# Opening part of an attention and two-MoE kernel: the sigmoids of a batch side by side, and a weight piece's last step behind the next piece's first

## The chip, the cores and the metric

One core of a Trainium2 chip runs the whole program. The metric is the device time of one execution in microseconds (us), taken as the median of several runs. The engines are named as the profile names them: PE (matrix products and transposes), ACT (activations and copies), DVE (elementwise work and reductions), POOL (elementwise work) and SP (it issues most DMAs).

## The reference

```python
def _attn_ref(q, k, v, M_prev, z_prev, beta):
    B, H, S, D = q.shape                       # 4, 8, 576, 64
    scores = np.matmul(q, k.transpose(0, 1, 3, 2)) / np.sqrt(D)   # causal mask, softmax -> a
    local = np.matmul(a, v)
    q_p = phi(q)                               # elu(q) + 1
    mem_out = einsum(q_p, M_prev) / (einsum(q_p, z_prev) + 1e-06)
    g = sigmoid(beta)
    return g * mem_out + (1 - g) * local

def _moe_ref(x, w_gate, w_val, w_out):         # x: 2304 x 512, weights 512 x 1536 and 1536 x 512
    return (sigmoid(x @ w_gate) * (x @ w_val)) @ w_out

def _moe2_ref(x, w_a, w_b, w_out):
    return ((x @ w_a) * (x @ w_b)) @ w_out

# out = moe2(moe(attention))
```

## The kernel before, in words

**Two parts.** The opening part (about the first 315 us) computes the attention for 16 pairs of heads, one pair after the other, and between the attention's instructions does part of the first MoE for the batches whose attention is done (`moe_a`, 4 of the 12 chunks of the hidden width). The late part computes the rest of both MoEs, with PE's order written out by hand. Its program is the same before and after the change.

**A pair.** The loop over `p` goes through a list of steps (`FIRST` for the first four pairs, `FIFTH`, then `LATER`). The steps that the text names are: the scores on PE (`scX`, `scY`, line 233); their masked copy with the row minimum on DVE (line 262) and the exponential on ACT (line 267), together `exX` and `exY`; transposes of q and k (line 180) with the copies out of PSUM, `kt` on ACT (line 176) and the put of `qt` on DVE (line 173); transposes of the probabilities (lines 368 and 380) with copies out of PSUM into `aw` on ACT (line 152); the product with v (`pv`, lines 398 and 404); and `M`, three or more products of the first MoE (lines 484 to 486, 492 to 494 after the change). All transposes and `pv` share three PSUM buffers named `tp`, so a copy out of PSUM that comes late holds PE. "Pair 4" below means the stretch on PE from the first score product of `p` = 4 to that of `p` = 5.

**The weights.** `w_stream` prepares 12 weight pieces of the first MoE, piece by piece. Each piece (`w_piece`) is a load of 512 KB into one of two buffers `st`, and then three steps: w1 (line 438 on DVE and 442 on ACT), w2 (lines 444 and 447 on DVE, then an integer add on POOL, line 450), and w3 (line 453 on ACT, which reads POOL's sum, then 454 on DVE, which reads ACT's result). Two buffers `wt` carry a piece from w1 to w3. A step `W` in the lists takes one step of the stream up to `p` = 3 and two from `p` = 4 on. The load of piece n+2 is issued in w3 of piece n.

**The sigmoids.** In `moe_a`, `gcopy` copies a chunk of the gate's product out of PSUM (line 527); after the fourth chunk two sigmoids of 128x1024 follow on ACT (line 530). The exponentials of the attention need another table of ACT, so a change of tables (`ACT_TABLE_LOAD`) stands before a sigmoid and again before the next exponential. `gat` (line 567) multiplies a chunk with its sigmoid.

**What sets the order.** In the opening part a scheduler orders each engine's instructions when the program is built, from the order of the code, its data dependencies and an estimate of when each instruction can run. Engines run their own list strictly in order.

Of the kernel before, what the change touches and what calls it, by code (L numbers as in the profile page):

```python
# [11 lines left out]
AF = mybir.ActivationFunctionType  # L12
# [7 lines left out]
def kernel(  # L20
# [31 lines left out]
    MA = 4  # L52
    PARTS = 9

    vec, act, pool, pe = nc.vector, nc.scalar, nc.gpsimd, nc.tensor
# [369 lines left out]
    def w_piece(wsrc, layer, c, kind, src):  # L425
        s = stp.tile([P, 512, 2], I32, tag="st", name="st")
        w32 = wsrc[kind].bitcast(I32)
        if kind == 2:
            nc.sync.dma_start(out=s.rearrange("p f t -> p (f t)"), in_=w32[c * P:(c + 1) * P, :])
        else:  # L430
            nc.sync.dma_start(
                out=s.rearrange("p (a f) t -> p a (f t)", a=KD),
                in_=w32[:, 2 * c * P:2 * (c + 1) * P].rearrange("(a p) f -> p a f", p=P),
            )
        yield
        hi, lo = s[:, :, 1], s[:, :, 0]
        c32 = work.tile([P, 512], I32, tag="wt", name="wt", bufs=NW)
        vec.tensor_scalar(
            out=c32.bitcast(F32), in0=hi.bitcast(F32), scalar1=2.0 ** -112, scalar2=None,
            op0=ALU.mult,  # L440
        )
        act.activation(out=lo, in_=lo.bitcast(U32), func=AF.Copy, scale=2.0 ** -29)
        yield
        vec.tensor_scalar(
            out=c32, in0=c32, scalar1=3, scalar2=None, op0=ALU.logical_shift_left
        )
        vec.scalar_tensor_tensor(
            out=c32, in0=hi, scalar=-(1 << 31), in1=c32, op0=ALU.bitwise_and, op1=ALU.bitwise_or
        )
        pool.tensor_tensor(out=c32, in0=c32, in1=lo, op=ALU.add)  # L450
        yield
        t = unit(src, f"w{kind}")
        act.activation(out=t[:, 0], in_=c32.bitcast(F32), func=AF.Copy)
        vec.tensor_tensor(
            out=t[:, 1], in0=c32.bitcast(F32), in1=t[:, 0].bitcast(F32), op=ALU.subtract
        )
        ws[layer, c, kind] = t
        yield

    def w_stream(pieces, ahead):  # L460

        gens = []
        pieces = iter(pieces)

        def more():
            a = next(pieces, None)
            if a is not None:
                g = w_piece(*a)
                next(g)
                gens.append(g)  # L470

        for _ in range(ahead):
            more()
        yield
        while gens:
            g = gens.pop(0)
            for i in range(3):
                next(g)
                if i == 2:
                    more()  # L480
                yield

    def mm3(o, w, ws_, xh, xl, first, last):
        pe.matmul(o, lhsT=w[:, 0, ws_], rhs=xh, start=first, stop=False, skip_group_check=True)  # L484
        pe.matmul(o, lhsT=w[:, 0, ws_], rhs=xl, start=False, stop=False, skip_group_check=True)  # L485
        return pe.matmul(  # L486
            o, lhsT=w[:, 1, ws_], rhs=xh, start=False, stop=last, skip_group_check=True
        )
# [16 lines left out]
    def moe_a(b):  # L505

        G, sg, gs, mo = {}, {}, {}, []  # L510

        def bank():
            return psm.tile([P, 512], F32, tag="m", name="m")

        def pairs():
            return work.tile([P, 2, 512], F32, tag="sg", name="sg", bufs=2)

        def half(c, kind, kk):
            if kk == 0:
                G[c] = bank()  # L520
            w, xs = ws[0, c, kind], xs_a[b, kk]
            mm3(G[c], w, slice(kk * P, kk * P + P), xs[:, 0], xs[:, 1], kk == 0, kk == KD - 1)

        def gcopy(c):
            if c % 2 == 0:
                sg[c // 2] = pairs()
            vec.tensor_copy(out=sg[c // 2][:, c % 2], in_=G[c])
            if c == MA - 1:
                for i in range(MA // 2):
                    act.activation(out=sg[i], in_=sg[i], func=AF.Sigmoid)  # L530

        def gat(c):
            gs[c] = gate(G[c], sg[c // 2][:, c % 2], 512)
            if c == MA - 1:
                finished.append(b)

        def outp(f, c):
            if c == 0:
                mo[:] = [bank()]
            mm3(mo[0], ws[0, c, 2], slice(f * P, f * P + P), *gs[c], c == 0, c == MA - 1)  # L540

        def fin(f):
            if f % 2 == 0:
                sg["io"] = pairs()
            io = sg["io"]
            if f % 2:
                act.activation(out=io[:, 1], in_=mo[0], func=AF.Copy)
                nc.sync.dma_start(out=x2d[b][:, f - 1:f + 1], in_=io)
            else:
                vec.tensor_copy(out=io[:, 0], in_=mo[0])  # L550

        for kind, then in ((0, gcopy), (1, gat)):
            for c in range(MA):
                for kk in range(KD):
                    yield (
                        b, (0, c, kind), partial(half, c, kind, kk),
                        partial(then, c) if kk == KD - 1 else None,
                    )
        for f in range(KD):
            for c in range(MA):  # L560
                yield (
                    b, (0, c, 2), partial(outp, f, c), partial(fin, f) if c == MA - 1 else None
                )

    def gate(vps, s, n, soon=False):

        st["gate"] = vec.tensor_tensor(
            out=s[:, 0:n], in0=vps[:, 0:n], in1=s[:, 0:n], op=ALU.mult
        )
        te = (dict(tag="gh", bufs=NG), dict(tag="gl", bufs=NG)) if NE is None else 2 * (dict(tag="e", bufs=NE),)  # L570
        gh = work.tile([P, 512], F32R, name="gh", **te[0])
        gl = work.tile([P, 512], F32R, name="gl", **te[1])
        rnd(gh[:, 0:n], s[:, 0:n], "g" in CD)
        (vec if soon else pool).tensor_tensor(
            out=gl[:, 0:n], in0=s[:, 0:n], in1=gh[:, 0:n].bitcast(F32), op=ALU.subtract
        )
        return gh, gl
# [43 lines left out]
    if True:  # L621
        start()
        wst = w_stream(
            [(w1, 0, c, kind, wp) for kind in range(3) for c in range(MA)],
            2,
# [1096 lines left out]
```

## Time and profile before

| what | value |
|---|---|
| median of 3 runs | 1053.35 us (1051.01 to 1054.12) |
| the profiled execution | 1052.07 us, of which its span is 1050.2 us |
| PE busy | 1025.6 us, 98% of the span |
| DVE, ACT, POOL busy | 736.7, 590.2, 188.8 us |
| granted clock of PE | 0.999 of full speed |

PE is the engine that the kernel's length hangs on. The 25 us by which it falls short of the span are the time that a faster order can win. Time on the other engines counts where PE waits for it.

### The profile page before, as it was taken

What the parts mean: (1) busy time and instruction counts of PE and PEld (TensorE: products, weight loads), DVE (VectorE), ACT (ScalarE), POOL (GpSimd) and SP (SyncE); (2) the same over time, 40 slices, a digit from 0 to 9 for tenths busy, and PEclk for the clock granted to TensorE, in tenths of its full rate; (3) what the DMA queues carried; (4) which work ended last, traced back from release to release, by engine and by line L of the source; (5) the groups of instructions that cost most, each with busy time, mean ns of one, the idle gap of its engine ahead of it and who ended that gap; (6) DMA issues with size and microseconds to landing.
All of it is one profiled execution on the core that took longest, in us unless ns stands there. A gap on an engine that the chain in (4) does not pass through costs nothing.

```text
span 1050.2 us, 17726 instructions
## 1 busy us (share of the span) xinstructions
PE 1025.6 (98%) x6158; PEld 859.0 (82%) x6158; DVE 736.7 (70%) x1589; ACT 590.2 (56%) x1276; POOL 188.8 (18%) x204
## 2 busy tenths in 40 slices
PE   7988999999999999999999999999999999999998
PEld 5656777777878988888888888888888888899998
DVE  6888755665627797765587558686586676898885
ACT  7888867867836556455654335454444545453432
POOL 2544521331211111110220000221121311000000
PEclk9999999999999999999999999999999999999999
DMA  7666434233215424332378754444352565644442
GB/s 174 155 180 161 135 89 125 81 87 85 60 54 172 161 82 149 102 130 79 118 267 285 237 169 161 130 136 136 95 190 91 189 231 182 216 141 143 144 125 72
DMA packets 154697, 150.14 MB, mean 143 GB/s; under 512 B 74608, under 2 KB 112624, under 8 KB 154608
## 3 DMA queue, kind: packets, MB, share of 16 engines
q1 hardware_dynamic: 152560, 148.16, 45.8%
q8 instruction: 48, 0.79, 0.3%
q10 hardware_dynamic: 2048, 0.86, 0.3%
q14 instruction: 41, 0.34, 0.1%
HBM read 103.29 MB, written 45.69 MB: 142 GB/s over the span
## 4 chain that ended last, share of the span: by engine, by line
PE 78%; DMA 6%; DVE 6%; ACT 5%; issue 2%; POOL 1%; SPq 1%; DVEq 0%; POOLq 0%; ACTq 0%
PE gv L485 16%; PE gv L486 16%; PE gv L484 16%; PE gv L1470 10%; PE m L484 3%; PE sc L233 3%; PE tp L404 3%; PE m L486 3%; PE m L485 3%; PE tp L368 2%; ACT s L267 1%; PE tp L398 1%; DMA xt<-xd 1%; PE tp L380 1%; DMA st<-in_moe_w_b_dram 1%
## 5 line engine op out<-in xcount | busy, mean ns | idle before, releaser
L484 PE MATMUL gv<-xm,w 128*128 128x512 f32 (+1 forms) x752 | 272.3, 362 | 0.5 <-ACT ev L1207 0.5
L486 PE MATMUL gv<-xm,w 128*128 128x512 f32 (+1 forms) x752 | 272.6, 363 | 0.0
L485 PE MATMUL gv<-xm,w 128*128 128x512 f32 (+1 forms) x752 | 272.6, 363 | 0.0
L925 POOL TENSOR_TENSOR wt<-wt,st 128x512 int32<-128x512 int32 x60 | 84.5, 1413 | 496.2 <-DVE wt L921 364.9
L484 PEld LDWEIGHTS gv<-xm,w 128*128 128x128 f32 x752 | 141.5, 188 | 23.4 <-ACT ev L1207 0.9
L485 PEld LDWEIGHTS gv<-xm,w 128*128 128x128 f32 x752 | 141.5, 188 | 22.6
L486 PEld LDWEIGHTS gv<-xm,w 128*128 128x128 f32 x752 | 141.6, 188 | 22.0
L1207 ACT ACTIVATE ev<-gv 128x512 f32<-128x512 f32 (+1 forms) x172 | 94.2, 562 | 79.4 <-PE gv L486 60.9
L1211 DVE TENSOR_TENSOR ev<-gv,ev 128x512 f32<-128x512 f32 x120 | 80.9, 684 | 64.4 <-PE gv L486 31.9
L1470 PE MATMUL gv<-wo,gs 128*128 128x256 f32 x1008 | 120.4, 282 | 0.5 <-DVE gs L1447 0.5
L1470 PEld LDWEIGHTS gv<-wo,gs 128*128 128x128 f32 x1008 | 120.2, 190 | 0.7 <-DVE gs L1447 0.7
L152 ACT ACTIVATE aw<-tp 128x512 f32<-128x512 f32 (+2 forms) x144 | 69.0, 507 | 46.3 <-PE tp L368 32.5
L262 DVE CUSTOM_DVE_ANT_0 s<-sc,mask 128x64 f32<-128x64 f32 (+4 forms) x160 | 69.0, 484 | 21.7 <-PE sc L233 21.6
L1446 ACT ACTIVATE gs<-ev 128x512 fp32r<-128x512 f32 (+1 forms) x96 | 50.9, 572 | 51.9 <-DMA ev<-gd 25.0
L915 ACT ACTIVATE wt<-st 128x512 f32<-128x512 f32 x60 | 39.7, 669 | 69.8 <-DMA st<-in_moe_w_out_dram 30.1
L267 ACT ACTIVATE s<-s,mx 128x320 f32<-128x320 f32 (+3 forms) x128 | 77.3, 607 | 2.7 <-DVE mx L262 2.7
L916 ACT ACTIVATE st<-st 128x512 int32<-128x512 uint32 x60 | 40.1, 669 | 37.8 <-DMA st<-in_moe_w_gate_dram 13.1
L486 PE MATMUL gv<-gs,w 128*128 128x512 f32 (+1 forms) x160 | 59.6, 373 | 0.0
L485 PE MATMUL gv<-gs,w 128*128 128x512 f32 (+1 forms) x160 | 59.4, 371 | 0.0
L484 PE MATMUL gv<-gs,w 128*128 128x512 f32 (+1 forms) x160 | 58.9, 368 | 0.0
L1447 DVE TENSOR_TENSOR gs<-ev,gs 128x512 fp32r<-128x512 f32 (+1 forms) x96 | 55.9, 615 | 3.1 <-ACT gs L1446 2.9
L233 PE MATMUL sc<-kt,qt 64*128 64x320 f32 (+4 forms) x468 | 54.2, 359 | 3.4 <-DVE mx L262 3.0
(158 smaller groups left out, 1828.5 us busy)
## 6 DMA issues: line engine op xcount, KB each, us to landing
gd<-ev SPq DMA_DIRECT2D x80, 256.0 KB
ev<-gd SPq DMA_DIRECT2D x80, 256.0 KB
st<-in_moe_w_out_dram SPq DMA_DIRECT2D x24, 512.0 KB
st<-in_moe_w_gate_dram SPq DMA_DIRECT2D x12, 512.0 KB
st<-in_moe_w_val_dram SPq DMA_DIRECT2D x12, 512.0 KB
st<-in_moe_w_a_dram SPq DMA_DIRECT2D x12, 512.0 KB
st<-in_moe_w_b_dram SPq DMA_DIRECT2D x12, 512.0 KB
x<-rd SPq DMA_DIRECT2D x32, 144.0 KB
```

Of the source, the lines that this page charges most:

```text
L152: act.activation(out=out, in_=src, func=AF.Copy)
L233: st["anchor"] = pe.matmul(scs[e][:, SC0[i] + a:SC0[i] + z], lhsT=x, rhs=y, start=n == 0, stop=n == len(terms) - 1, skip_group_check=True,)
L262: st["pace"] = vec.tensor_tensor_reduce(out=s, in0=scs[e][:, SC0[i]:SC0[i] + w], in1=mask[:, c:c + w], scale=1.0, scalar=BIG, op0=ALU.add, ...
L267: st["apace"] = act.activation(out=o, in_=s, func=AF.Exp, scale=-1.0, bias=mx[:, i:i + 1], accum_out=sms[p % 2][:, i:i + 1, e],)
L484: pe.matmul(o, lhsT=w[:, 0, ws_], rhs=xh, start=first, stop=False, skip_group_check=True)
L485: pe.matmul(o, lhsT=w[:, 0, ws_], rhs=xl, start=False, stop=False, skip_group_check=True)
L486: return pe.matmul(o, lhsT=w[:, 1, ws_], rhs=xh, start=False, stop=last, skip_group_check=True)
L925: pool.tensor_tensor(out=c32, in0=c32, in1=lo, op=ALU.add)
L1207: act.activation(out=t[:, 0:n], in_=src[:, 0:n], func=func)
L1211: st["gate"] = vec.tensor_tensor(out=t, in0=src, in1=t, op=ALU.add)
L1447: vec.tensor_tensor(out=t[:, 1, 0:n], in0=f[:, 0:n], in1=t[:, 0, 0:n].bitcast(F32), op=ALU.subtract,)
L1470: st["gate"] = pe.matmul(mo[i][:, 256 * r:256 * r + 256], lhsT=t[:, th, q_], rhs=w[:, wl_, wc:wc + 256], start=first and not r and not z, ...
```

## The change

Two edits. The first: after the fourth `gcopy` of a batch, the first of the two sigmoids now also waits for that `gcopy`, so that both stand next to each other. The second: `w_stream` yields its steps in another order. Before it was w1, w2, w3 of piece n, then of piece n+1. Now it is w1(0), w2(0), then w1(n+1), w3(n) with the load of n+2, w2(n+1) for each n. There are 37 steps in both.

```diff
         for _ in range(ahead):
             more()
         yield
+
+        for i in (0, 1):
+            next(gens[0])
+            yield
         while gens:
             g = gens.pop(0)
-            for i in range(3):
-                next(g)
-                if i == 2:
-                    more()
+            if gens:
+                next(gens[0])
+                yield
+            next(g)
+            more()
+            yield
+            if gens:
+                next(gens[0])
                 yield
...
-            vec.tensor_copy(out=sg[c // 2][:, c % 2], in_=G[c])
+            last = vec.tensor_copy(out=sg[c // 2][:, c % 2], in_=G[c])
             if c == MA - 1:
+
                 for i in range(MA // 2):
-                    act.activation(out=sg[i], in_=sg[i], func=AF.Sigmoid)
+                    a = act.activation(out=sg[i], in_=sg[i], func=AF.Sigmoid)
+                    if i < MA // 2 - 1:
+                        tc.add_manual_dep(
+                            a.ins, last.ins.name,
+                            mybir.DependencyInfo(
+                                mybir.DependencyClass.Sync, mybir.DependencyReason.DATA
+                            ),
+                            reason="one table",
+                        )
```

**What moves.** The built programs hold the same instructions on every engine, but for six `ACT_TABLE_LOAD` fewer on ACT (three before a sigmoid, three before an exponential). The order differs in the first 7 pairs, and for ACT also around the sigmoids of the two later batches; behind that all lists are the same. Lines above 480 have another number after the change (530 becomes 539, 527 becomes 535, 503 becomes 511).

ACT around the first sigmoid of the first batch, at the seam of pairs 5 and 6, before the change (`sg` is the gate, `mix` the first exponential of the next pair):

```order
L152 ACTIVATE aw<-tp 128x320 x2
L284 ACTIVATE e<-e 128x640
L152 ACTIVATE aw<-tp 128x512
L530 ACT_TABLE_LOAD
L530 ACTIVATE sg<-sg 128x1024
L267 ACT_TABLE_LOAD
L267 ACTIVATE mix,sm_93<-s_1355,mx 128x64
```

ACT after the change, in pair 6, where the second sigmoid of the batch stood before:

```order
L442 ACTIVATE st<-st 128x512
L176 ACTIVATE kt<-tp 128x448
L152 ACTIVATE aw<-tp 128x320
L539 ACT_TABLE_LOAD
L539 ACTIVATE sg<-sg 128x1024 x2
L152 ACTIVATE aw<-tp 128x320
L284 ACT_TABLE_LOAD
```

The first sigmoid and its two changes of tables have left the seam of the pairs; the two sigmoids stand between one pair of changes in pair 6, ahead of an `aw` copy.

DVE in pair 4 at `exY`, before the change (`w_977` is the weight piece whose w3 this is):

```order
L438 TENSOR_SCALAR wt<-st 128x512
L503 TENSOR_TENSOR xs<-x,xs 128x512
L454 TENSOR_TENSOR w_977<-wt,w_977 128x512
L262 ISA s,mx<-sc,mask 128x192
```

The same place after the change (the piece's number is now `w_980`), from the end of `exY` on:

```order
L262 ISA s,mx<-sc,mask 128x576
L262 ISA mx 128x1
L444 TENSOR_SCALAR wt<-wt 128x512
L300 TENSOR_REDUCE nr<-e 128x10
L454 TENSOR_TENSOR w_980<-wt,w_980 128x512
L173 TENSOR_SCALAR qt<-tp 128x448
L447 SCALAR_TENSOR_TENSOR wt<-st,wt 128x512
```

The w3 that stood in front of `exY` now stands behind it, between w2's first operation and the put of `qt`.

DVE in pair 5 behind `exY`, before the change:

```order
L262 ISA s,mx<-sc,mask 128x576
L262 ISA mx 128x1
L300 TENSOR_REDUCE nr<-e 128x10
L438 TENSOR_SCALAR wt<-st 128x512
L173 TENSOR_SCALAR qt<-tp 128x448
```

And after it:

```order
L300 TENSOR_REDUCE nr<-e 128x10
L535 COPY sg<-m 128x512
L438 TENSOR_SCALAR wt<-st 128x512
L173 TENSOR_SCALAR qt<-tp 128x448
```

A `gcopy` that stood ahead of `exY` now stands behind it, ahead of the put of `qt`.

## Rows read from the trace of the kernel before

**Rows 1.** The page's span, and its busy time of each engine.

```profile
span 1050.2 us, 17726 instructions
PE 1025.6 (98%) x6158; PEld 859.0 (82%) x6158; DVE 736.7 (70%) x1589; ACT 590.2 (56%) x1276; POOL 188.8 (18%) x204
```

**Rows 2.** Stretches of 25 us: length, then busy time of each engine.

```profile
core 0: us, PE busy (x) PEld busy (x) DVE busy (x) ACT busy (x) POOL busy (x), PEclk, DMA share, GB/s
50.00:75.00 25.00, 21.81 (x181) 14.68 (x177) 21.68 (x70) 21.83 (x62) 11.15 (x15) 1.00 0.67 178
75.00:100.00 25.00, 20.93 (x142) 14.89 (x139) 20.16 (x52) 20.57 (x53) 11.76 (x14) 1.00 0.64 170
100.00:125.00 25.00, 24.16 (x167) 18.33 (x167) 19.56 (x56) 22.51 (x54) 11.06 (x12) 1.00 0.51 142
125.00:150.00 25.00, 25.00 (x167) 19.52 (x166) 19.05 (x54) 18.84 (x53) 10.57 (x14) 1.00 0.35 98
```

**Rows 3.** The same view, cut at the pairs' first score products: pairs 2 to 7.

```profile
29.06:42.24 13.18, 11.06 (x87) 7.45 (x86) 10.87 (x36) 11.17 (x34) 6.30 (x8) 1.00 0.66 155
42.24:54.67 12.43, 11.75 (x101) 8.36 (x100) 10.95 (x36) 11.72 (x36) 5.71 (x8) 1.00 0.66 161
54.67:69.76 15.09, 12.58 (x102) 8.53 (x102) 12.38 (x42) 14.40 (x42) 5.72 (x10) 1.00 0.69 181
69.76:89.69 19.93, 17.32 (x119) 12.04 (x118) 18.44 (x50) 14.52 (x39) 10.78 (x11) 1.00 0.67 188
89.69:112.55 22.86, 20.88 (x147) 15.94 (x146) 18.69 (x53) 20.95 (x46) 10.31 (x12) 1.00 0.53 144
112.55:132.20 19.65, 19.34 (x134) 14.71 (x133) 14.47 (x39) 16.71 (x45) 10.27 (x12) 1.00 0.45 126
```

**Rows 4.** PE's timeline: start, length, what; in brackets idle time before it.

```profile
34.75 1.57 PE L233 MATMUL sc<-kt,qt 64*128 64x192 f32 x12 [0.84 <-DVE mx L262]
...
69.18 0.66 PE L368 MATMUL tp<-ident,s 128*128 128x128 f32 x4 [1.15 <-DVE qt L173]
...
80.20 0.49 PE L485 MATMUL m<-xs,w 128*128 128x512 f32 x1 [0.94 <-DVE xs L503]
...
89.10 0.66 PE L380 MATMUL tp<-ident,mix 128*128 128x128 f32 x4 [1.30 <-DVE qt L173]
...
96.25 0.76 PE L398 MATMUL tp<-aw,mv 128*64 128x320 f32 x4 [1.45 <-ACT aw L152]
...
114.65 0.33 PE L180 MATMUL tp<-ident,kn 128*128 128x128 f32 x1 [0.31 <-ACT aw L152]
```

**Rows 5.** ACT's timeline in pairs 5 and 6, and its group of loads before sigmoids.

```profile
74.45 0.63 ACT L453 ACTIVATE w<-wt 128x512 fp32r<-128x512 f32 x1 [2.43 <-POOL wt L450]
...
91.28 1.28 ACT L530 ACT_TABLE_LOAD   x1
92.58 1.06 ACT L530 ACTIVATE sg<-sg 128x1024 f32<-128x1024 f32 x1
93.65 1.28 ACT L267 ACT_TABLE_LOAD   x1
94.95 0.35 ACT L267 ACTIVATE mix<-s,mx 128x64 f32<-128x64 f32 x1
...
L530 ACT ACT_TABLE_LOAD x6 | 7.7, 1283 | 0.1
```

**Rows 6.** Weight steps on DVE and POOL, and a weight load on SP's queue.

```profile
64.57 0.69 DVE L454 TENSOR_TENSOR w<-wt,w 128x512 fp32r<-128x512 f32 x1 [1.78 <-ACT w L453]
83.23 1.46 DVE L447 SCALAR_TENSOR_TENSOR wt<-st,wt 128x512 int32<-128x512 int32 x1
109.74 0.74 DVE L438 TENSOR_SCALAR wt<-st 128x512 f32<-128x512 f32 x1 [0.26 <-DMA st<-in_moe_w_out_dram]
...
82.86 1.29 POOL L450 TENSOR_TENSOR wt<-wt,st 128x512 int32<-128x512 int32 x1
...
105.94 0.36 SPq L429 DMA_DIRECT2D st<-in_moe_w_out_dram x1
```

## The prediction

> **What bounds the kernel now.** I read the page first. PE is busy 1025.6 of 1050.2 us [rows 1], so over the whole program some 25 us are to be won at most, whatever the other engines save. Then the busy times by stretch, to see where those 25 us lie. From 125 us on PE is busy 25.00 of 25.00; in 50 to 125 us it is idle for 3.19, 4.07 and 0.84 us, together 8.1 [rows 2]. Cut at the pairs the same view gives PE's idle time as 2.12, 0.68, 2.51, 2.61, 1.98 and 0.31 us in pairs 2 to 7 [rows 3]. No engine is full there: in pair 4 ACT is busy 14.40 of 15.09 us, in pair 5 DVE 18.44 of 19.93, in pair 6 ACT 20.95 of 22.86 [rows 3]. So pairs 2 to 6 are bound by chains of waits that go from engine to engine, and from pair 7 on by PE alone.
>
> Then PE's own timeline, for what ended each idle time. Six of them carry the argument: 0.84 us at 34.75 for the score copies on DVE, 1.15 at 69.18 and 1.30 at 89.10 for the put of `qt` on DVE, 0.94 at 80.20 for a split on DVE, 1.45 at 96.25 and 0.31 at 114.65 for `aw` copies on ACT [rows 4]. Last the engines that were late. ACT idled 2.43 us at 74.45 in front of w3, until POOL's sum came; and at 91.28 to 94.95 it changed tables, did a sigmoid and changed back before the first exponential of pair 6 could start [rows 5]. DVE idled 1.78 us at 64.57 in front of its half of a w3, with `exY` of pair 4 queued behind [rows 6]. The change touches these three places.
>
> **The change part by part.** The sum is made against the profiled execution, 1052.07 us, which is 1.28 below the median of the runs shown, so I subtract it from the median at the end.
>
> The instructions are the same but for six changes of tables. At 1.283 us each [rows 5] ACT gets 7.7 us of free time. Four of the six belong to the second and third batch, which fall behind 125 us, where PE idles nowhere and ACT is busy 18.84 of 25 us [rows 2]. PE's own products hide those, and I count them as nothing; without that cover they would be worth 2.57 us for each batch. The first sigmoid of those batches now comes up to 1.06 us nearer to the product that needs it; the same cover holds, and I take nothing there too.
>
> *Pair 2.* The new order puts DVE's half of w3 behind `exX` and not in front. It takes 0.69 us, as the one at 64.57 [rows 6]. PE's idle 0.84 us at 34.75 ended on just these copies. I take 0.6 us; the bounds are 0 (another copy is late instead) and 0.84.
>
> *Pair 4.* The w3 that waited 1.78 us now stands behind `exY` on DVE, so `exY` and the put of `qt` behind it come earlier, and PE's 1.15 us at 69.18 should go. But ACT has only 15.09 - 14.40 = 0.69 us free in this pair, and what is late next is its `aw` copy. I take 0.5 us; the bounds are 0 and 1.15.
>
> *Pair 5.* With w2 and w3 of a piece no longer in one `W`, POOL has the time of another step for its sum, and ACT's 2.43 us go. The split behind it (0.94 us of PE at 80.20) comes in time. The 1.30 us at 89.10 stay, and grow: a `gcopy`, one DVE pass over 128x512 like w3 (0.69), now stands ahead of the put of `qt`, and PE's transposes of `mix` wait for that put with 12 products behind them. I take 0.94 - 0.69, some 0.3 us. The bounds are -0.7 (only the new wait) and 0.94 + 1.30 = 2.24.
>
> *Pair 6.* The seam loses two changes and a sigmoid, 1.28 + 1.06 + 1.28 = 3.62 us [rows 5], ahead of the first exponential. PE's wait of 1.45 us at 96.25 is for an `aw` copy behind them, and goes. The other end of the pair gets 1.06 us more in front of an `aw` copy, since two sigmoids stand between the changes there. ACT comes to that place with the 3.62 us in hand, but PE comes earlier as well, so I take the wait of 0.31 at 114.65 as little changed, some 0.05 more. That gives 1.4 us; the bounds are 1.45 - 1.06 = 0.4 and 1.45 + 0.31 = 1.8.
>
> The load of a weight piece is issued at the w3 of the piece two before it, as before, but w1 of its own piece now comes two steps later and not four, which from pair 4 on is one `W` and not two. The nearest row is the last load: issued at 105.94, and w1 at 109.74 still waited 0.26 us for it [rows 6], so a load takes 3.8 us. A pair has three or four `W` in 15 to 23 us [rows 3], some 5 us each. The load fits with about 1 us to spare, and I count it as nothing; what it costs if not is a rival below. SP no longer has to wait for POOL at that load, since the buffer is free a step earlier; no wait of SP shows on PE, so this too is nothing.
>
> Sum: 0.6 + 0.5 + 0.3 + 1.4 = 2.8 us, with -0.3 and 6.0 as the sums of the bounds. The late part has the same order on each engine and starts from the same tiles, so it only shifts. 1052.07 - 2.8 = 1049.3 for an execution like the profiled one, 1053.35 - 2.8 = 1050.55 for the median.
>
> The Trainium skill, ScalarE: Activation LUTs, section What ACT_TABLE_LOAD costs, counts about 2.66 us for a switch, 1.28 for the load and 1.38 for a drain. By that figure the seam would lose 6.4 and not 3.62 us, ACT would have 2.8 us more in hand, and the first rival below would be the likeliest, with its 1047.4. The trace disagrees: the load begins at 91.28 and the sigmoid at 92.58, and no second part lies between them or ahead of the load [rows 5].
>
> **The rivals.**
>
> *Most of PE's idle time goes.* ACT and DVE run ahead by their freed waits (2.43 and 1.78 us) and by the 3.62 us of the seam, and each next pair finds its copies done. For it: no engine is full in pairs 5 and 6. Against it: the put behind `gcopy`, and ACT in pair 4. At most 2.51 + 2.61 + 1.98 = 7.1 us [rows 3]; I take 6, which gives 1047.4.
>
> *The gain is given back by POOL.* An operation on DVE next to a POOL add takes longer: the w2 at 83.23 took 1.46 us with the add of 82.86 to 84.15 running [rows 6], against the 0.69 of a w3 alone. Before, w3(n) waited for the add of its own piece, so it never ran beside it. Now w3(n) stands right behind w2(n+1) on DVE, whose add starts on POOL just then: so in pairs 2, 4, 5 and 6, once each. That is up to 4 x 0.77 = 3.1 us on DVE, and it cancels the 2.8: 1053.6, no change. Against it: where DVE's next operation waits anyway, nothing is lost. The Trainium skill, SBUF — State Buffer, section Who interferes with whom, has the reason: a DVE operation with two inputs in SBUF and a POOL operation that reads SBUF keep each other out for a whole instruction. The trace agrees in that one row.
>
> *Slower: w1 waits for its load.* The lead is one `W`. Where the load is late, DVE stands still in w1, and behind it in order stand a w3 and `exX` of the next pair. DVE has 19.93 - 18.44 = 1.49 us free in pair 5 [rows 3]; beyond that PE waits. Three w1 stand in that stretch; at 1.5 us late each they hold DVE 4.5 us, which puts PE back by 3.0 and takes the gains of pairs 5 and 6 as well: 1053.35 - 1.1 + 3.0 = 1055.3. It decides from a load of some 5.5 us on, against the 3.8 seen. Against it: loads before had two `W`, and only one of them was waited for.
>
> **How the numbers follow.** The forecast, a gain of 1.5 to 4.2 us around 2.8 (1049.1 to 1051.9), gets 0.45. Most idle time gone: 0.20. Given back: 0.25. Slower: 0.10. About 0.3% (3.2 us) is what a measurement can tell from no change. The first rival lies beyond it, and so does somewhat under half of the forecast's range, 0.2, together 0.40 for faster. Slower by that much is the larger half of the last rival and the tail of the one before it, 0.09. The rest, 0.51, is within. The range for 8 in 10 reaches from most of the first rival, 1047.0, to beyond no change, 1054.6; it leaves out about 0.1 on either side.
>
> **What would show it.** In the profile after: three loads of tables in front of sigmoids and not six; no wait of ACT for POOL's sum near 2.4 us; pair 4's `exY` on DVE ending about 2 us earlier; the first exponential of pair 6 about 3 us or more earlier; PE's idle of 1.45 us before `pv` gone; a wait of about 2 us for the put of `qt` in pair 5; and the first score product of pair 8 some 2.8 us before 132.20. It is wrong if w1 on DVE shows waits for its DMA, if w3 on DVE takes 1.4 us in most places, or if behind 132 us the shift grows or is lost.

## The result and the profile after

The changed kernel took 1058.46 us (median of 6 runs, 1056.87 to 1059.42) against 1053.03 us (6 runs) of the kernel before on the same chip: a ratio of 1.0057, 95% interval 1.0046 to 1.0067, so 5.4 us slower. The prediction said 1050.55, in a range that ended at 1054.6, and gave "slower" 0.09.

The page after, the lines that answer to [rows 1]:

```profile
span 1057.2 us, 17716 instructions
PE 1030.4 (97%) x6158; PEld 862.8 (82%) x6158; DVE 736.7 (70%) x1589; ACT 582.5 (55%) x1270; POOL 188.7 (18%) x204
```

ACT lost the 7.7 us of six table loads, as costed. PE is busy 4.8 us longer with the same 6158 instructions, which points to time at a lower clock. The stretches after, cut as [rows 3] into pairs 2 to 7 (the third number from the end is the granted clock), then a part of pair 5, then pairs 8 to 14 together:

```profile
29.21:42.02 12.81, 11.01 (x87) 7.45 (x86) 10.40 (x35) 10.79 (x33) 5.71 (x8) 1.00 0.72 187
42.02:55.26 13.24, 12.09 (x103) 8.57 (x102) 12.62 (x41) 12.50 (x38) 6.01 (x9) 1.00 0.53 127
55.26:70.63 15.37, 12.56 (x100) 8.33 (x100) 13.52 (x42) 13.56 (x40) 7.34 (x10) 1.00 0.70 186
70.63:94.63 24.00, 19.77 (x122) 14.59 (x121) 20.49 (x52) 16.40 (x43) 10.07 (x12) 0.86 0.59 162
94.63:116.94 22.31, 20.83 (x138) 15.90 (x137) 16.58 (x45) 15.62 (x39) 8.67 (x11) 1.00 0.47 123
116.94:137.76 20.82, 20.82 (x139) 15.42 (x138) 14.70 (x41) 17.83 (x45) 11.12 (x13) 1.00 0.47 130
...
78.64:85.47 6.83, 5.79 (x18) 4.70 (x19) 6.64 (x17) 5.00 (x17) 2.17 (x3) 0.50 0.74 174
...
137.76:274.85 137.09, 136.67 (x1011) 106.16 (x1010) 81.22 (x258) 93.48 (x261) 34.90 (x52) 1.00 0.34 94
```

The same stretch in the kernel before:

```profile
132.22:269.31 137.09, 136.67 (x1009) 106.16 (x1009) 81.03 (x258) 99.61 (x266) 34.88 (x52) 1.00 0.34 94
```

Set against [rows 3], pairs 2 to 7 changed by -0.37, +0.81, +0.28, +4.07, -0.55 and +1.17 us, together +5.41. Pairs 8 to 14 are 137.09 us in both, so in the opening part everything happened before pair 8. Behind pair 14, where the order is the same, the two profiles differ by another 1.46 us (780.89 and 782.35); two profiles of one and the same program differ as much there (780.89 and, in e4 below, 779.54), so I read nothing from that part.

In this profile most of the loss is in pair 5; a second profile of the same program (e3 below) spreads it otherwise. In pair 5 PE is idle 24.00 - 19.77 = 4.23 us instead of 2.61, and busy 2.45 us longer. Pairs 6 and 7 do not hold the same work in both kernels: PE has 138 and 139 instructions there after the change and had 147 and 134 before, so these two are better taken together (+0.62).

What PE waited for in pair 5, from the timelines of PE, DVE, ACT and POOL after (start, length, what; idle time in brackets):

```profile
79.68 0.90 PE L368 MATMUL tp<-ident,s 128*128 128x128 f32 x3 [3.60 <-DVE qt L173]
80.80 0.63 PE L493 MATMUL m<-xs,w 128*128 128x512 f32 x1
81.23 0.63 PE L494 MATMUL m<-xs,w 128*128 128x512 f32 x1
...
73.97 1.90 DVE L287 SCALAR_TENSOR_TENSOR qp<-qn,e 128x640 f32<-128x640 f32 x1 [0.51 <-POOL mix L326]
...
77.01 1.17 DVE L454 TENSOR_TENSOR w<-wt,w 128x512 fp32r<-128x512 f32 x1 [0.78 <-ACT w L453]
78.10 0.21 DVE L262 CUSTOM_DVE_ANT_0 s<-sc,mask 128x64 f32<-128x64 f32 x1
...
79.34 0.28 DVE L173 TENSOR_SCALAR qt<-tp 128x128 f32<-128x128 f32 x1
...
75.79 0.67 ACT L442 ACTIVATE st<-st 128x512 int32<-128x512 uint32 x1 [3.08 <-DMA st<-in_moe_w_val_dram]
...
73.90 1.28 POOL L450 TENSOR_TENSOR wt<-wt,st 128x512 int32<-128x512 int32 x1
76.01 1.62 POOL L290 TENSOR_TENSOR e<-qp,zb 128x640 f32<-128x640 f32 x1 [0.82 <-issue]
```

The same place before, on DVE:

```profile
73.18 0.22 DVE L262 CUSTOM_DVE_ANT_0 s<-sc,mask 128x64 f32<-128x64 f32 x1
...
75.73 0.28 DVE L173 TENSOR_SCALAR qt<-tp 128x128 f32<-128x128 f32 x1
...
76.49 0.81 DVE L287 SCALAR_TENSOR_TENSOR qp<-qn,e 128x640 f32<-128x640 f32 x1
```

Before, DVE did `exX` and the put of `qt` (128 columns) first, and `qp` and w1 behind them. After, `qp`, w1 and a w3 stand ahead of `exX` in DVE's list. The put comes 79.34 - 70.63 = 8.71 us into the pair and not 75.73 - 69.76 = 5.97, and PE, whose MoE products now stand behind the transposes that need that buffer, idles 3.60 us. From 78.64, some 2.6 us into that wait, the granted clock is 0.50 (1.2 GHz) for 6.83 us: products follow each other in 0.43 us (80.80 to 81.23) and not in 0.23 as before.

The chain of waits in that place (start, length, what):

```profile
69.70 1.52 POOL wt L450
...
71.24 4.47 DMA st<-in_moe_w_val_dram
...
75.79 0.67 ACT st L442
...
77.01 1.17 DVE w L454
...
79.42 0.21 DVE qt L173
```

It reads like the third rival: a weight load that starts when POOL's sum frees its buffer, and w1 (here ACT's half) waiting 3.08 us for it. That was my first theory (A, in later runs L), and it fell. Its rival B, that the order of the steps itself costs, was made more precise on the way: P for PE's order, D for DVE's and ACT's.

### The profile page after: what moved, and what is told of

Read it like the earlier page. It is cut to its first block, busy times and chain, and to the rows that moved or that the text cites. A ratio compares the mean times of both kernels' runs of the same rounds, so it can differ in the third digit from the quotient of the medians.

```text
span 1057.2 us, 17716 instructions
## 1 busy us (share of the span) xinstructions
PE 1030.4 (97%) x6158; PEld 862.8 (82%) x6158; DVE 736.7 (70%) x1589; ACT 582.5 (55%) x1270; POOL 188.7 (18%) x204
## 4 chain that ended last, share of the span: by engine, by line
PE 79%; DVE 6%; DMA 5%; ACT 5%; issue 2%; SPq 2%; POOL 1%; ACTq 0%; DVEq 0%; POOLq 0%
PE gv L494 16%; PE gv L493 16%; PE gv L492 16%; PE gv L1487 8%; PE m L492 3%; PE m L494 3%; PE m L493 3%; PE sc L233 3%; PE tp L368 3%; PE tp L404 3%; ACT s L267 2%; PE tp L398 1%; DMA ev<-gd 1%; DMA xt<-xd 1%; PE tp L380 1%
```

## The experiments

"Before" is the median of the kernel before in the same set of runs; its level differs by up to 1 us from set to set, so the ratios are what to compare.

| run | median | before | ratio, 95% interval |
|---|---|---|---|
| e1 sigmoids only | 1052.11 | 1051.83 | 1.0003 (0.9995 to 1.0012) |
| e2 stream only | 1056.66 | 1051.83 | 1.0045 (1.0031 to 1.0059) |
| e3 load issued earlier | 1057.56 | 1051.83 | 1.0052 (1.0039 to 1.0066) |
| e4 before, load issued later | 1051.45 | 1051.83 | 0.9999 (0.9990 to 1.0007) |
| e5 third buffer | 1057.14 | 1052.42 | 1.0042 (1.0029 to 1.0055) |
| e6 after, PE's order of before | 1055.23 | 1052.42 | 1.0022 (1.0010 to 1.0033) |
| e7 before, PE's order of after | 1054.51 | 1052.42 | 1.0020 (1.0009 to 1.0031) |
| e8 gap filled | 1060.44 | 1052.42 | 1.0072 (1.0055 to 1.0088) |
| e9 after, scores' chain first | 1055.27 | 1051.34 | 1.0036 (1.0023 to 1.0049) |
| e10 as e9, and PE in pair 5 | 1055.50 | 1051.34 | 1.0041 (1.0028 to 1.0054) |
| e11 before, scores' chain late | 1054.09 | 1051.34 | 1.0025 (1.0017 to 1.0034) |
| e12 before, sigmoids held | 1052.12 | 1051.34 | 1.0001 (0.9992 to 1.0010) |
| e13 before, moves as costed | 1050.10 | 1052.54 | 0.9984 (0.9975 to 0.9992) |
| e14 as e13, copies ahead | 1051.60 | 1052.54 | 0.9992 (0.9983 to 1.0000) |
| e15 as e14, puts ahead | 1050.40 | 1052.54 | 0.9978 (0.9968 to 0.9987) |
| e16 as e9, scores together | 1055.52 | 1052.54 | 1.0029 (1.0019 to 1.0039) |
| e17 as e13, puts ahead | 1049.03 | 1052.03 | 0.9979 (0.9969 to 0.9989) |

**Which edit: e1 and e2.** Each is one hunk of the change's diff alone.

> Only the first edit: the two sigmoids of a batch side by side, the weight stream in the order of before. Theory A (in the new stream a weight piece's load has a lead of one W and not two, w1 waits for it on ACT and DVE, PE idles 3.6 us in pair 5 and then runs at a lower clock): the loss is not here, and the seam of pairs 5 and 6 gives what pair 6 gave after the change or my forecast of it, 0.5 to 1.4 us, so 1051.6 to 1052.5 against 1053.0. Rival C (two sigmoids in one place hold ACT 1.06 us longer in front of an aw copy, and PE's products slip behind transposes): the loss of 5.4 us shows here, 1056 to 1058.5.

> Only the second edit: the weight stream in the new order, the sigmoids as before. Theory A (lead of one W): the whole loss and none of the seam's gain, 1058.5 to 1060, with PE's idle time of about 3.6 us in pair 5 and a stretch at the lower clock behind it. Rival B (the order of the three steps itself costs, w3 next to POOL's add and ahead of the copies): the same 1058.5 to 1060, this run does not tell A from B. Rival C (the sigmoids): 1052 to 1054.

The loss is the stream's (e2 has 4.8 of 5.4 us, by medians), and C falls. e2 lies below the range that A and B shared, though its interval overlaps that of the change. The sigmoids alone gained nothing either. Pairs 6 and 7 of e1:

```profile
90.03:110.96 20.93, 20.41 (x143) 15.52 (x142) 17.52 (x52) 17.01 (x43) 10.15 (x12) 1.00 0.54 153
110.96:133.25 22.29, 20.95 (x138) 15.49 (x137) 15.24 (x40) 18.40 (x46) 10.82 (x12) 1.00 0.43 115
```

Pair 6 is 1.93 us shorter than in [rows 3], more than the 1.4 costed, and pair 7 is 2.64 longer. Part of both is that four of PE's transposes went from the end of pair 6 into pair 7 (143 and 138 instructions, not 147 and 134). In pair 7 PE waits for a put that waited for ACT's `kt` copy:

```profile
121.41 0.55 PE L368 MATMUL tp<-ident,s 128*128 128x128 f32 x3 [1.34 <-DVE qt L173]
```

**The load's lead: e3, e4 and e5.**

```diff
         for i in (0, 1):
             next(gens[0])
+            if i:
+                more()
             yield
...
             next(g)
-            more()
             yield
             if gens:
                 next(gens[0])
+                more()
                 yield
```

> Both edits, but the load of piece n+2 is issued right behind w2 of piece n, two steps earlier than after the change, so that the lead is again four steps (two W). Steps and their order are those after the change. Theory A (the lead): the wait of 3 us of ACT and DVE for the load in front of w1 goes, PE's 3.6 us in pair 5 and the slow stretch too, and the forecast of the prediction comes up: 1050.5 to 1052.5. Rival B (the order of the steps): the load changes nothing, 1057 to 1058.5. Between them a load that SP now issues while it waits for POOL's add, with other transfers queued behind it: 1053 to 1056.

> The kernel before with one thing changed: the load of piece n+2 is issued in w2 of piece n+1 and not in w3 of piece n, two steps later, so that w1 has a lead of one W as after the change. Order of the steps and sigmoids as before. Theory A (the lead): w1 waits for its load here too, PE idles in pairs 4 to 7, 1055.5 to 1059. Rival B (the order of the steps): within 1 us of before, 1052 to 1054.

Neither tells anything about the lead: the built programs are those of after (e3) and of before (e4), instruction for instruction on every engine. Here the scheduler issues a load when its buffer is free, wherever the code asks for it. They stand as second measurements of the two kernels, and as such they show something that one profile cannot. In e4 the kernel before repeats its pairs: none of pairs 2 to 7 differs from [rows 3] by more than 0.04 us. In e3 the changed kernel does not. Its pairs 2 to 5:

```profile
29.37:43.38 14.01, 12.15 (x86) 8.36 (x85) 11.33 (x39) 11.82 (x35) 6.31 (x9) 0.92 0.66 172
43.38:57.16 13.78, 12.62 (x103) 8.96 (x102) 11.75 (x36) 11.62 (x36) 5.33 (x8) 0.96 0.55 138
57.16:73.21 16.05, 13.22 (x100) 8.84 (x99) 14.19 (x42) 14.24 (x41) 7.93 (x10) 0.96 0.63 172
73.21:96.39 23.18, 19.83 (x122) 14.47 (x121) 20.86 (x52) 15.83 (x42) 9.55 (x11) 0.88 0.56 163
```

Against [rows 3] that is +0.83, +1.35, +0.96 and +3.25 us. Pair 5 is again the largest, but 3.1 us lie ahead of it, where the profile after had 0.7. The granted clock was 0.50 in three stretches of 3.41 us (from 41.08, 71.80 and 82.04), two of them at places where it stayed at 1.00 in the profile after. So a difference of a microsecond in one pair of the changed kernel, between two single profiles, says little.

What sets the lead is the buffer, so e5 gave every third piece a buffer of its own:

```diff
-        s = stp.tile([P, 512, 2], I32, tag="st", name="st")
+        nst[0] += 1
+        if nst[0] % 3:
+            s = stp.tile([P, 512, 2], I32, tag="st", name="st")
+        else:
+            s = work.tile([P, 512, 2], I32, tag="st3", name="st", bufs=1)
...
-            2,
+            3,
```

> Both edits, and every third weight piece of the opening is loaded into a third buffer st, with three loads ahead, so that a load no longer waits for POOL's sum of the piece before last. Theory L (w1 waits for its load, because in the new order the buffer comes free only three steps before the w1 that needs it): the waits of ACT and DVE for st in pair 5 go, the put of qt there comes 1.5 to 3 us earlier, pair 5 shrinks from 24.0 to 20.5 to 22 us, 1054 to 1056. Theory P (the order that the scheduler gives PE after the change is at fault: in pair 5 nine products of the MoE that stood ahead of or between the transposes stand behind the first three of them): the load wait goes, but PE still idles for the put, 1056 to 1058.5.

ACT and DVE in pair 5 of e5, which begins at 71.92:

```profile
76.05 0.64 ACT L458 ACTIVATE w<-wt 128x512 fp32r<-128x512 f32 x1 [1.92 <-POOL wt L455]
...
76.96 2.03 DVE L459 TENSOR_TENSOR w<-wt,w 128x512 fp32r<-128x512 f32 x1
...
80.15 0.28 DVE L173 TENSOR_SCALAR qt<-tp 128x128 f32<-128x128 f32 x1
```

No wait for `st` is left there. But the next instruction of the same list waits 1.92 us for POOL's sum, DVE's w3 runs 2.03 us beside a POOL operation, and the put still comes 8.23 us into the pair. The time is in the range of P, and A falls: the load was only the wait that ended last among several on instructions that now stand ahead of `exX`.

**PE's order: e6 and e7.** A chain of dependencies holds PE's 284 instructions between pairs 3 and 7 in a given order; in e6 the changed kernel gets the order of before, in e7 the kernel before gets that of after. Only PE is held: in answer the scheduler also moved some copies, puts and weight steps on ACT and DVE in that stretch, so neither run changes PE's order alone.

```diff
+        turn = [pes[a + k] for a, n in PE_ORDER for k in range(n)]
+        for a, b in zip(turn, turn[1:]):
+            tc.add_manual_dep(b, a.name, ...)
```

> Both edits, but PE's instructions in pairs 3 to 7 are held in exactly the order that they had before the change; the other engines keep the new streams, except where the scheduler now places an instruction a little otherwise. Theory P (PE's order): pair 5 comes back to 20 to 21.5 us, no slow clock, and the gains of the forecast show: 1050.5 to 1053.5. Theory L (the load): DVE's put of qt stays at its late place, nine products of 0.23 us fill 2.1 of PE's 3.6 us, the rest stays idle: 1055 to 1057.

> The kernel before, but PE's instructions in pairs 3 to 7 are held in exactly the order that they have after the change; weight stream and sigmoids are those of before. Theory P (PE's order): most of the loss without either edit, 1054.5 to 1058. Theory L (the load): the put of qt in pair 5 is as early as before, so PE loses at most 1 us there: 1051.5 to 1053.

Pair 5 of e6 and PE's wait in it, then pairs 3, 5 and 6 of e7 and PE's longest wait in its pair 5:

```profile
71.15:92.22 21.07, 18.19 (x118) 13.27 (x117) 19.26 (x49) 14.52 (x39) 10.09 (x11) 0.92 0.61 173
```

```profile
80.64 0.55 PE L377 MATMUL tp<-ident,s 128*128 128x128 f32 x3 [2.68 <-DVE qt L182]
```

```profile
41.87:55.09 13.22, 12.10 (x103) 8.57 (x102) 11.75 (x38) 12.54 (x38) 5.87 (x9) 1.00 0.63 150
69.83:91.28 21.45, 17.50 (x122) 12.40 (x121) 20.53 (x55) 15.90 (x42) 11.02 (x12) 1.00 0.62 176
91.28:112.62 21.34, 20.81 (x138) 15.91 (x137) 15.95 (x48) 19.12 (x41) 9.63 (x12) 1.00 0.58 148
```

```profile
85.66 0.52 PE L389 MATMUL tp<-ident,mix 128*128 128x128 f32 x3 [2.08 <-POOL wt L459]
```

With PE's order of after, and what the scheduler moved along with it, pair 3 is as long as after (13.22 against 13.24). Pair 5 is 1.5 us longer, but not at the put of 128 columns: PE's longest wait there is in the second half of the pair, and pair 6, with nine instructions fewer, is 1.5 us shorter. The kernel is 2.1 us slower by the medians, at the lower edge of P's range. e6 came out in the range of L: with PE's old order the put is as late as after (9.15 us into the pair), and PE waits 2.68 us for it. Pair 5 is only 1.14 us longer than in [rows 3] there, and pairs 4 and 6 are 1.62 and 1.64 longer. So PE's order has a part in the loss and is not the whole, and the parts cannot be added up pair by pair.

**The clock: e8.** Fourteen products fill the wait; PE's order is held otherwise.

```diff
             w, xs = ws[0, c, kind], xs_a[b, kk]
+            if (b, c, kind, kk) == (0, 0, 0, 0):
+                for _ in range(14):
+                    pe.matmul(G[c], lhsT=w[:, 0, 0:P], rhs=xs[:, 0], start=True, stop=True, ...)
```

> Both edits, with 14 more products of 128x512 on PE in pair 5, ahead of the three transposes that wait for the put of qt; their result is overwritten by the first real product. The rest of PE's order is held as after the change. They take 14 x 0.232 = 3.2 us, which is less than the wait of 3.60 us. Theory C (the idle time itself lets PE's granted clock fall to half afterwards, and that is 2.4 of the 4.1 us that pair 5 lost): the clock stays at 1.0, pair 5 takes 21.3 to 22 us, 1055.5 to 1056.5. Rival (the clock falls for another reason, or its price is not on the path): pair 5 stays at 23.5 to 24.5 us, 1057.5 to 1059.

```profile
70.48:94.09 23.61, 20.93 (x136) 15.05 (x135) 21.23 (x53) 16.51 (x43) 10.95 (x12) 1.00 0.55 156
```

```profile
79.80 0.55 PE L377 MATMUL tp<-ident,s 128*128 128x128 f32 x3 [0.47 <-DVE qt L182]
...
88.24 0.52 PE L389 MATMUL tp<-ident,mix 128*128 128x128 f32 x3 [1.43 <-POOL wt L459]
```

With the wait filled down to 0.47 us the clock stayed at 1.00, which fits that the idle time let it fall; it is one execution. The pair is 0.39 us shorter than in the profile after, less than what the two executions of the changed kernel differ by there (24.00 and 23.18), so what the clock cost isn't measured; a wait of 1.43 us further on is one place where the speed was given back. The run as a whole was slower than after, outside both ranges: behind pair 14 its profile is 785.00 us long, 2.65 longer than after. Why is not shown.

**DVE and ACT: e9, e10 and e11.** From here on all engines are held. `HELD` lists for each engine the instructions of the opening in their order of before or after; unchanged, it builds the same order again, and an experiment moves only single names in it.

```python
def hold(nc, tc):
    by = {i.name: i for i in nc.cur_bb.bb.instructions}
    for names in HELD.values():
        turn = [by[f"I-{n}"] for n in names.split() if f"I-{n}" in by]
        for a, b in zip(turn, turn[1:]):
            tc.add_manual_dep(b, a.name, ...)
```

e9, DVE and then ACT (in the changed kernel; `exX` has eight rows):

```diff
+L262 ISA s_1096,mx<-sc,mask 128x64
...
+L173 TENSOR_SCALAR qt<-tp 128x128
 L287 SCALAR_TENSOR_TENSOR qp<-qn,e 128x640
 L438 TENSOR_SCALAR wt<-st 128x512
 L454 TENSOR_TENSOR w_1080<-wt,w_1080 128x512
-L262 ISA s_1096,mx<-sc,mask 128x64
...
-L173 TENSOR_SCALAR qt<-tp 128x128
...
-L442 ACTIVATE st<-st 128x512
-L453 ACTIVATE w_1080<-wt 128x512
 L267 ACTIVATE mix,sm_94<-s_1096,mx 128x64
 L176 ACTIVATE kt<-tp 128x128
 L267 ACTIVATE mix,sm_94<-s_1099,mx 128x64
+L442 ACTIVATE st<-st 128x512
+L453 ACTIVATE w_1080<-wt 128x512
```

> Both edits, every engine held in its order after the change up to about pair 9, with one thing moved: in pair 5 exX and the put of qt on DVE stand ahead of qp, w1 and the second w3 again, and on ACT the two exponentials of mix and the kt copy ahead of the half of w1 that waits for its load, as before the change. Theory D (what costs in pair 5 is that the scheduler placed the weight steps ahead of the attention's own chain on DVE and ACT, so that every wait and every slow instruction of theirs delays the put): the put comes at about 75 us instead of 79.34, PE's 3.60 us go, pair 5 takes 20 to 22 us, 1054 to 1056. Theory L (the load and POOL are late in any place): the wait moves to the copies behind, pair 5 stays above 23 us, 1057 to 1058.5.

```profile
72.67:93.45 20.78, 18.50 (x122) 13.11 (x121) 17.39 (x48) 14.80 (x40) 9.56 (x11) 0.95 0.59 167
```

```profile
72.67 2.85 PE L233 MATMUL sc<-kt,qt 64*128 64x64 f32 x12
...
76.82 0.29 DVE L173 TENSOR_SCALAR qt<-tp 128x128 f32<-128x128 f32 x1
77.02 0.82 DVE L287 SCALAR_TENSOR_TENSOR qp<-qn,e 128x640 f32<-128x640 f32 x1
```

The put comes 4.15 us into the pair, the wait of 3.60 us is gone, and the pair is 3.22 us shorter than in the profile after, though its first products ran at the lower clock in this profile (2.85 us for 12, against 1.78). Theory D held for the pair, and 1055.27 lies in its range. The load is as late as after: ACT's half of w1 starts 4.94 us into the pair, having waited for it, and after the change 5.16. It holds no put now:

```profile
77.61 0.69 ACT L442 ACTIVATE st<-st 128x512 int32<-128x512 uint32 x1 [0.84 <-DMA st<-in_moe_w_val_dram]
...
87.82 0.52 PE L380 MATMUL tp<-ident,mix 128*128 128x128 f32 x3 [1.50 <-POOL wt L450]
```

Two things limit what this run shows. Further on in the pair PE now waits 1.50 us, put down to POOL's sum, where it had no such wait after. And the kernel is still 1.0036 of before, 3.8 us, where the change as a whole was 1.0057: by these ratios some 2.2 us came back. Pairs 2 to 4, which have the same order as after on every engine, were together 2.9 us longer than in [rows 3] in this profile.

> As the run before, and in pair 5 PE's instructions are in their order of before the change too: nine MoE products ahead of and between the transposes. Theory P, as a part beside D: another 0.5 to 1.5 us, 1053 to 1055. If PE's order matters only while the put is late: no difference from the run before.

With the put on time, PE's order in pair 5 makes no difference that these intervals can show.

e11 is the converse, in the kernel before: on DVE the second w3, w1 and `qp` stand ahead of `exX` and the put.

> The kernel before, every engine held in its order, with one thing moved: in pair 5 exX and the put of qt on DVE stand behind the second w3, w1 and qp, as after the change. Weight stream, PE's order and the sigmoids are those of before. Theory D: the put comes 2 to 3.5 us later, PE's nine products ahead of it cover about 2 us, pair 5 is 1 to 3 us longer, 1053.5 to 1055.5. Theory L: nothing above 0.5 us, 1052 to 1053.

```profile
70.11:92.37 22.26, 18.48 (x118) 13.36 (x118) 18.79 (x50) 14.50 (x39) 10.75 (x11) 0.92 0.62 167
```

```profile
79.17 0.90 PE L368 MATMUL tp<-ident,s 128*128 128x128 f32 x3 [2.26 <-DVE qt L173]
```

Pair 5 is 2.33 us longer than in [rows 3] and the kernel 1.0025 of before (interval above), with neither edit in it and nothing moved but these three instructions of DVE. The clock fell here too (0.92 in the pair).

**The terms of my sum: e12 and e13.** In the kernel before, held, e12 moves only each first sigmoid next to the second; e13 also moves the w3 of pair 2 behind `exX` and that of pair 4 behind `exY`. e13 on DVE in pair 4 (`exY` has eight rows):

```diff
+L262 ISA s,mx<-sc,mask 128x192
...
+L444 TENSOR_SCALAR wt<-wt 128x512
+L300 TENSOR_REDUCE nr<-e 128x10
 L454 TENSOR_TENSOR w_977<-wt,w_977 128x512
-L262 ISA s,mx<-sc,mask 128x192
...
-L444 TENSOR_SCALAR wt<-wt 128x512
-L300 TENSOR_REDUCE nr<-e 128x10
```

> The kernel before, every engine held in its order, with only the first sigmoid of each batch moved on ACT to stand right before the second: six changes of tables fewer, and nothing else moves. If the seam was costed rightly and what the first edit alone gave back in pair 7 came from the scheduler's other moves: pair 6 is 1.4 to 2 us shorter and it stays, 1050.2 to 1051.2. Rival (two sigmoids in a row in front of an aw copy cost in pair 7 what the seam gives): 1052 to 1053.

Pairs 6 and 7 of e12, and PE's wait in pair 7:

```profile
89.06:110.43 21.37, 20.86 (x147) 15.95 (x146) 18.12 (x53) 17.42 (x43) 10.67 (x12) 1.00 0.57 156
110.43:131.03 20.60, 19.37 (x134) 14.71 (x133) 14.63 (x39) 17.96 (x46) 10.26 (x12) 1.00 0.44 117
```

```profile
113.44 0.33 PE L180 MATMUL tp<-ident,kn 128*128 128x128 f32 x1 [1.23 <-ACT aw L152]
```

The seam gives 1.49 us (1.4 costed). In pair 7 the wait of 0.31 [rows 4] became 1.23: the joined sigmoids' 1.06 us stand in front of that copy nearly whole. Net 0.54 us, too little to measure, so the rival of this run was right.

> The kernel before, every engine held in its order, with only the moves that the prediction costed: the sigmoids of a batch side by side, the w3 of pair 2 behind exX and the w3 of pair 4 behind exY on DVE. If the terms were right and the loss came from moves that I had not costed: pair 2 shorter by 0.4 to 0.6 us, pair 4 by 0.3 to 0.5, pairs 6 and 7 together by 0.55 as in the run with the sigmoids alone, so 1.2 to 1.7 us below before. If the terms were wrong in themselves: within 0.6 us of before.

```profile
54.41:68.48 14.07, 12.57 (x102) 8.53 (x101) 12.50 (x41) 13.42 (x40) 5.89 (x9) 1.00 0.74 194
```

Pair 4 is 1.02 us shorter (0.5 costed), and pair 5 behind it 0.30 longer (20.23). Together the moves make the kernel faster: 0.9984 (0.9975 to 0.9992), some 1.7 us. The moves that were costed for pairs 2, 4 and 6 are a gain; the change as the scheduler built it is a loss. Pair 5's term is not among the moves of this run.

**A version that beats both: e14, e15 and e17.** e14 moves two `aw` copies on ACT ahead of the change of tables back, to spare pair 7 its wait. e15 adds the put of `qt` (448 columns) right behind `exY` in pairs 4 and 5, ahead of w2, `nr` and w1. e17 is e15 without e14's move. e14's move on ACT, then e15's on DVE in pair 5:

```diff
+L152 ACTIVATE aw<-tp 128x512 x2
 L284 ACT_TABLE_LOAD
 L284 ACTIVATE e<-e 128x640
 L442 ACTIVATE st<-st 128x512
 L453 ACTIVATE w_1583<-wt 128x512
-L152 ACTIVATE aw<-tp 128x512 x2
...
+L173 TENSOR_SCALAR qt<-tp 128x448
 L300 TENSOR_REDUCE nr<-e 128x10
 L438 TENSOR_SCALAR wt<-st 128x512
-L173 TENSOR_SCALAR qt<-tp 128x448
```

> As the run before it, and on ACT in pair 6 the two aw copies of 128x512 stand right behind the sigmoids and the aw copy, ahead of the change of tables back, e, and the halves of w1 and w3. If the wait of 1.23 us in pair 7 is for ACT's work in that place: it goes, 1 to 1.3 us below the run before it, 2.2 to 3 us below before. If something else is late there: no difference.

> As the run before it, and on DVE in pairs 4 and 5 the put of qt with 448 columns stands right behind exY, ahead of w2, nr and w1. PE waited 1.15 and 1.30 us for these two puts before. If the cause found carries over (weight steps ahead of a put cost PE): 0.8 to 2.2 us below the run before it. If ACT's copies are late there next: within 0.5 us of it.

> The moves as costed (1050.1 alone) and the two puts of qt ahead of the weight steps, without the ACT copies that were moved in between, since those gave nothing. If the puts are worth by themselves what they gave before (1.2 us): 1048.5 to 1049.5 against 1052 to 1052.5, a ratio of 0.9965 to 0.998. If they only made up for the moved copies: the same as the moves as costed, 0.998 to 0.9985.

e14 fell: the 1.23 us went, and in pair 7 PE waited 0.78 us for a put and 0.76 for an `aw` copy instead. e15 and e17 are some 2.2 us faster than the kernel before, and so than both (intervals above); that e17 is better than e13 alone can't be told from these intervals.

**A rest: e16.** In the order of e9, pair 7's two score products of 448 columns stand side by side again, with the four transposes behind them.

> As the run in which the scores' chain of pair 5 is moved back in the changed kernel (1055.3), and in pair 7 the two score products with 448 columns, one of each head, stand next to each other on PE again, with the four transposes behind them. Together they took 1.78 us with the others in the profile before, apart the second takes 1.02 by itself. Theory P: pair 7 is 0.5 to 1.0 us shorter, 1054.3 to 1054.9. Rival (the transposes' copies are then late by as much): no difference, 1055.0 to 1055.6.

Pair 7 lost 0.3 us (20.82 to 20.53 by the same view), and 1.0029 can't be told from e9's 1.0036: its rival was right. e16 has e9's order in pair 5 as well, and its profile, the longest of its eleven executions, took 22.87 us there (20.78 in e9, 20.64 in e10), with the granted clock at 0.83. What is the same in all three is the first half: the score products of 192 columns come 10.4 to 11.3 us into the pair, against 15.51 after and 14.06 in e3.

## Why the prediction was wrong

**The step that failed is the term of pair 5.** I put it at a gain of 0.3 us, from POOL's sum that would come in time, less a `gcopy` ahead of the other put of `qt`. It measured a loss of 4.07 us in the profile after and 3.25 in e3. I looked at the rows of DVE at the pair's end and not at those between `exX` and the put of 128 columns, where the list had changed more: w1, a w3 and `qp` had moved ahead of both, and the put came 2.74 us later. e9 and e11 show it from either side with few moves: 3.22 us less in the pair when they are moved back, 2.33 more when they are moved there in the kernel before. The wait that I had costed for the pair's end, the 1.30 us growing to 2, isn't in the profile after: PE's longest wait behind that place is 0.53 us, for an `aw` copy.

**That is not the whole loss.** The sum had no term for pair 3, and took pair 7 as nearly unchanged. Pair 3 is 0.8 us longer in the profile after and in e7, so that goes with PE's order and what moved along with it. Pairs 2 and 4, costed as gains, came out between -0.37 and +0.83, and between +0.28 and +0.96 us, in two executions of the same program. With pair 5's chain moved back (e9) the kernel was still 3.8 us slower than before, and no run shows which moves cost that.

**The load counted as nothing.** It was late as the third rival said, and that rival's time (1055.3) came nearest. My reasons were wrong twice: the buffer is not free a step earlier, since the load began as POOL's sum ended (71.23), and it took 4.47 us, not 3.8. But it is not by itself the cause: without the wait (e5) the loss stayed, and with the load as late (e9) pair 5's wait for the put went.

**POOL beside DVE.** The second rival's mechanism is in the trace: `qp` took 1.90 us beside POOL and 0.82 in e9 clear of it, a w3 1.17 and in e5 2.03, against 0.69 alone. That agrees with the rule of the Trainium skill, SBUF — State Buffer, section Who interferes with whom, that a DVE instruction with two inputs in SBUF contends with a POOL instruction that reads SBUF. In pair 5 after the change these two rows add some 1.6 us to DVE ahead of the put (1.08 and 0.48), an estimate from the rows; no run took POOL away, so its price in the whole is not measured.

**Pair 6.** The mechanism and the size were right (1.49 in e12 against 1.4). The other end, "little changed, some 0.05 more", was mis-sized: 0.92.

**Pairs 2 and 4.** Pair 4 was right in sign and, taken alone, under-sized (1.02 for 0.5 in e13; 0.72 with what pair 5 lost behind it). After the change it didn't show, since PE's and ACT's orders had changed there too (+0.28). Pair 2's term of 0.6 is not borne out: with its move the pair took 12.91 us in e13, and without it 12.80 in e12, where nothing had moved there. The 0.37 us of the profile after can't be told from that, nor from e3's +0.83.

**Batches 2 and 3 counted as nothing** was right: pairs 8 to 14 have the same length to 0.01 us.

**Open:** which moves cost what is left in e9 (3.8 us), why the clock falls in pairs 2 to 4 in some executions of the changed kernel and not in others, and why the late part, with the same order everywhere, takes from 779.5 to 785.0 us in these profiles.

## What to carry to other kernels

Where a scheduler orders the instructions, an edit of one stream moves others too: print the order of every engine between each pair of waits that bounds the time, and cost what moved ahead of the critical chain, not the edit. Holding the order and moving single instructions tells the worth of the moves one had in mind (here -1.7 us) from what the scheduler adds to them (5.4 + 1.7, an estimate of 7.1 us from two sets of runs), and then keeps the gain. A wait that ends last need not be the cause: if instructions beside it in the same list end just earlier, taking it away gains nothing (e5, e14). And one profile of a kernel need not be typical: take two before reading a microsecond out of a stretch (e3 against after).

## What the runs showed of the hardware

PE's granted clock fell to 0.50 (1.2 GHz) some 2.6 us into an idle 3.60 us and stayed there for 6.83 us, and stayed at 1.00 when products filled the gap (e8). It also fell in other executions behind shorter waits: behind 2.26 us in e11, and in e3 at 41.08, where PE's wait just before was 0.43 us. What it cost is not shown; the 2.45 us more that PE was busy in pair 5 also hold three instructions more.

Where a w3, the second operation of w2 or `qp` on DVE ran into a POOL operation that had begun before it, it ended just behind that operation: `qp` at 75.87 and POOL's sum at 75.18, a w3 at 78.18 and POOL's product at 77.63, in e5 a w3 at 78.99 and POOL's product at 78.44. The distance was 0.55 to 0.69 us in these three, about what such an operation takes alone (0.69 and 0.82), so it lost nearly what POOL still had to do.
